# A state-space layer pair on one core: the taps' angle and magnitude matmuls read 128 rows, with zeros for the half that isn't theirs

## The chip, the cores and the metric

The kernel runs on one core of one Trainium2 chip. The time is device microseconds of that core, from launch to end, and the median of several runs counts. The profile is one further execution, taken by the hardware profiler. Its span is the time from the core's first instruction to its last.

A core has five engines with an instruction stream each: TensorE (PE, matmuls; its weight loads are shown apart as PEld), VectorE (DVE), ScalarE (ACT), GpSimd (POOL) and SyncE (SP, which here issues most transfers). Each works through its stream in order. TensorE's clock is granted by a gate, at half or full speed; the profile shows the granted share as PEclk.

## The reference, cut to what matters

The input is a sequence x of 2048 steps and 512 channels. Four layers follow each other, A, B, A, B, each on the layer norm of x and added to x:

```python
def A(q, k, v, shift_k, ssm_k, ssm_D):
    kv = shift_conv(k, shift_k) * v            # 4 taps
    return q * (causal_conv(kv, ssm_k) + kv * ssm_D)

def B(u, log_A_real, A_imag, C_real, C_imag, log_dt, D_skip):
    dt = exp(log_dt)                           # per channel d
    A = -exp(log_A_real) + 1j * A_imag         # [512 channels, 128 modes]
    C = (C_real + 1j * C_imag) * dt
    K[d, l] = 2 * sum_n Re(C[d, n] * exp(A[d, n] * dt[d] * l))
    return causal_conv(u, K) + u * D_skip
```

A's convolution doesn't depend on x (only its gate q does), and both layers A share it, as both layers B share the kernel K. So the filter K, called the taps here, has to be made once: 512 channels of 2048 values, each a sum over 128 modes.

## The kernel before, in words

The long convolutions are Fourier transforms written as matmuls. `fwd_group` with `fwd_rows` (L173) does the first step into a PSUM tile `pf`, VectorE transposes it (L191, L193), and `f2_chunk` (L198) does the second into `pu`. A filter's spectrum is copied out (`pc`, L249) and sent to DRAM as `spec`, by `spectrum_quarter`, a quarter of the channels at a time. `convolution` multiplies by it (L283 to L288) and goes back by L297 and L318.

The taps are made by `taps`, in 64 steps n = 4 gi + k: 16 groups gi of 32 channels, and in each group four steps k of 8 channels. Step k is split as `h, s = divmod(k, 2)`. All mode parameters are held as three 2-byte parts of each number with a fourth part of zero. `load_rows` brings a group's `rows` from DRAM: 128 rows for each h, of which rows 0 to 63 belong to the eight channels of s = 0 and rows 64 to 127 to those of s = 1. A matmul of these rows (128 modes as output partitions) with a small table (`tt`, `tg1`, `tg2`) gives 512 columns, one phase or exponent for each channel and position:

- `mags` (L486, `pm`): exponents. For `col == 2` it uses all 128 rows and table `tg2`, 16 channels at once; otherwise the 64 rows of one s and table `tg1`. ScalarE takes the exponential (L492, `m`).
- `angles` (L501, `pa`): phases by table `tt`, from the 64 rows of one s. VectorE rounds them to whole turns (L505, `y`), and L506 subtracts these on TensorE with the matrix `minus`.
- `waves` (L512 to L514): sine and cosine on ScalarE, in place in `pa` and into `co`.
- `products` (L524 to L528): wave by magnitude, on GpSimd and VectorE, into `xye`.
- `contract` (L538): sums over the modes by 32-column matmuls into `pk`; after four steps L547 and L548 scale the result, and it goes to DRAM as `kdram`.

`pm` and `pa` share three PSUM banks (NPA = 3). Exponentials are made for two groups at a time, so that ScalarE changes its tables seldom.

Two streams run together: `stream` (taps, and each quarter's spectrum of K as soon as 16 steps are done), one step at a time, and `diagonal`, two steps at a time. `diagonal` first makes the spectrum of A's filter in four quarters (`kk` from `ssmk_in`; the A transposes L191 write `x`), beside it the product kv on GpSimd (L636) and VectorE (L644, L646), and the row statistics (L655), and then runs A's convolution. The stage ends near 412 us; after it come A's gate, layer B, the second gate and the second layer B.

The order in which the instructions are written down is not the order in which they stand: a scheduler puts each engine's stream in order by its own model of what would be ready when. So a change of shape in one instruction can move others.

Of the kernel before, what the change touches and what calls it, by code (L numbers as in the profile page):

```python
# [79 lines left out]
def mode_constants():  # L80
    m = np.arange(32)
    n2 = np.concatenate([32 + m, 31 - m])
    tabs = {
        "tt": (8, np.concatenate([m + 1, 64 * m + 32]), np.repeat([0, 1], 32)),
        "tg1": (8, n2, 0 * n2),
        "tg2": (16, 64 * m, 0 * m + 1),
    }
    out = {}
    for name, (chans, rate, off) in tabs.items():
        t = np.zeros((2, 2, 8, 4, chans, len(rate)), np.float32)  # L90
        for s in range(2):
            for c in range(8):
                for r, factors in enumerate((rate, off)):
                    t[s, r, c, :3, (8 * s + c) % chans] = factors
        out[name] = t.reshape(128, chans, len(rate))
    out["minus"] = -np.eye(128, dtype=np.float32)
    return out
# [3 lines left out]
def kernel(ctx: ExitStack, tc: tile.TileContext, out, x_in, kv_in, ssmk_in, ssmd_in,  # L101
# [323 lines left out]
    split(3, t2, V)  # L425
    S.activation(warm, t2[:, 0, 0:1], AF.Exp, scale=0.0)
    tabs = {}
    for key, c_, w_, src in (("tg2", 16, 32, tg2_in), ("tg1", 8, 64, tg1_in), ("tt", 8, 64, tt_in)):
        tabs[key] = gp.tile([128, c_, w_], BF16, name=key)
        G.dma_start(tabs[key], src)  # L430
    nc.sync.dma_start(flat(dt2), ldtb_in[:, None, :].to_broadcast([4, 32, 128]))
# [35 lines left out]


    NR = 3
    rows, ms, pks, angs = {}, {}, {}, {}  # L470
    NM = 5
    last_exp, last_sin = [None], [None]
# [8 lines left out]

    def mags(gi, k, col):
        h, s = divmod(k, 2)
        hs = slice(0, 128) if col == 2 else slice(64 * s, 64 * s + 64)
        pm = pp.tile([128, 512], F32, name="pm", tag="pa", bufs=NPA)
        T.matmul(pm, rows[gi][hs, 1, h, :], tabs["tg2" if col == 2 else "tg1"][hs], start=True, stop=True)  # L486
        if col == 2:
            ms[gi, h] = wk.tile([128, 16, 96], F32, name="m", tag="m", bufs=NM)
            m = ms[gi, h][:, :, 64:96]
# [6 lines left out]

    def angles(gi, k):
        h, s = divmod(k, 2)
        hs = slice(64 * s, 64 * s + 64)
        pa = pp.tile([128, 512], F32, name="pa", tag="pa", bufs=NPA)  # L500
        T.matmul(pa, rows[gi][hs, 0, h, :], tabs["tt"][hs], start=True, stop=False,  # L501
                 skip_group_check=True)

        y = wk.tile([128, 512], F16, name="y", tag="y", bufs=2)
        V.tensor_scalar(y, pa, MAGIC, MAGIC, op0=ALU.add, op1=ALU.subtract)  # L505
        T.matmul(pa, minus, y, start=False, stop=True, skip_group_check=True)  # L506
        angs[gi, k] = pa
# [465 lines left out]
```

## Time and profile before

| | us |
|---|---|
| median of 3 runs | 711.91 |
| lowest and highest | 708.33, 714.90 |
| the profiled execution's own time | 715.19 |
| its span | 713.4 |
| TensorE busy (PE) | 574.0 |
| TensorE weight loads (PEld) | 392.5 |
| VectorE busy (DVE) | 522.5 |
| ScalarE busy (ACT) | 486.4 |
| GpSimd busy (POOL) | 461.5 |

The mean granted clock of TensorE was 0.935. A row of the profile reads: line, engine, operation, tile written <- tiles read, shapes, count, then busy time in us and the mean of one in ns, then idle time of the engine just before and what ended it. In a matmul's shape, `64*128` is rows by columns of the array in use, and `64x512` the moving operand. A matmul of 4-byte numbers shows as two records. A row of the timeline starts with start and length in us. A row of the windows gives from:to, length, then busy time and count of instructions of PE, PEld, DVE, ACT and POOL, the granted clock, the share of the transfer engines' time and GB/s.

### The profile page before, as it was taken

What the parts mean: (1) busy time and instruction counts of PE and PEld (TensorE: products, weight loads), DVE (VectorE), ACT (ScalarE), POOL (GpSimd) and SP (SyncE); (2) the same over time, 40 slices, a digit from 0 to 9 for tenths busy, and PEclk for the clock granted to TensorE, in tenths of its full rate; (3) what the DMA queues carried; (4) which work ended last, traced back from release to release, by engine and by line L of the source; (5) the groups of instructions that cost most, each with busy time, mean ns of one, the idle gap of its engine ahead of it and who ended that gap; (6) DMA issues with size and microseconds to landing.
All of it is one profiled execution on the core that took longest, in us unless ns stands there. A gap on an engine that the chain in (4) does not pass through costs nothing.

```text
span 713.4 us, 14266 instructions
## 1 busy us (share of the span) xinstructions
PE 574.0 (80%) x4984; PEld 392.5 (55%) x4984; DVE 522.5 (73%) x947; ACT 486.4 (68%) x886; POOL 461.5 (65%) x483
## 2 busy tenths in 40 slices
PE   1276876788898999989988977987898718689996
PEld 0043544445576786756745565766576304566783
DVE  7835878976585775674774878476797898988875
ACT  3435566658769868797898567986566375696572
POOL 5534989978758596595795522077668502787783
PEclk9999888967989999999999989999999959999999
DMA  8456968774773757746474795568786240577682
GB/s 285 164 168 203 348 210 289 234 252 146 231 223 105 206 137 191 214 131 196 125 206 138 218 325 168 177 177 240 190 220 169 64 123 1 147 182 213 194 224 103
DMA packets 84555, 134.44 MB, mean 188 GB/s; under 512 B 16892, under 2 KB 33924, under 8 KB 83332
## 3 DMA queue, kind: packets, MB, share of 16 engines
q1 hardware_dynamic: 83268, 131.01, 61.6%
q0 software_dynamic: 1216, 2.52, 1.4%
q8 instruction: 39, 0.64, 0.4%
q14 instruction: 32, 0.26, 0.1%
HBM read 98.28 MB, written 35.65 MB: 188 GB/s over the span
## 4 chain that ended last, share of the span: by engine, by line
PE 43%; ACT 15%; DVE 15%; DMA 13%; issue 7%; POOL 5%; SPq 2%; DVEq 0%; ACTq 0%; POOLq 0%
PE pu L198 15%; PE pf L173 11%; PE pi L297 6%; DMA kab<-spec 4%; PE po L318 4%; PE pk L538 3%; ACT u L818 2%; PE pm L486 2%; DMA spec<-pc 2%; POOL sw L287 2%; DVE x L755 2%; ACT co L514 1%; ACT sw L283 1%; PE pa L506 1%; DVE vv L285 1%
## 5 line engine op out<-in xcount | busy, mean ns | idle before, releaser
L287 POOL TENSOR_TENSOR sw<-sw,kab 128x512 f32<-128x512 f32 x96 | 125.7, 1315 | 70.2 <-ACT sw L284 58.7
L285 DVE TENSOR_TENSOR vv<-pu,kab 128x512 f32<-128x512 f32 x96 | 64.9, 679 | 67.1 <-ACT sw L284 46.2
L297 PE MATMUL pi<-vv,mm 128*128 128x128 f32 x768 | 104.2, 280 | 7.2 <-DVE vv L285 5.0
L297 PEld LDWEIGHTS pi<-vv,mm 128*128 128x128 f32 x768 | 93.9, 192 | 21.4 <-issue 11.2
L288 POOL TENSOR_TENSOR vv<-vv,sw 128x512 f32<-128x512 f32 x76 | 98.9, 1306 | 9.2 <-DVE vv L285 6.4
L283 ACT ACTIVATE sw<-pu 64x512 f32<-64x512 f32 x96 | 57.0, 594 | 61.7 <-PE pu L198 57.1
L173 PE MATMUL pf<-kk,wz 128*128 128x256 f32 (+1 forms) x176 | 64.0, 616 | 40.6 <-issue 17.3
L524 POOL TENSOR_TENSOR xye<-co,m 128x512 f32<-128x512 f32 x64 | 75.7, 1183 | 23.6 <-ACT co L514 15.2
L636 POOL TENSOR_TENSOR term<-kvt 128x512 f32<-128x512 f32 x64 | 81.9, 1299 | 12.0 <-ACT acc L642 9.0
L198 PE MATMUL pu<-x,w 128*128 128x128 f32 x512 | 81.3, 307 | 8.2 <-ACT pc L249 5.4
L198 PEld LDWEIGHTS pu<-zu,w 128*128 128x128 f32 x512 | 62.6, 190 | 43.1 <-DVE vv L285 17.6
L198 PEld LDWEIGHTS pu<-x,w 128*128 128x128 f32 x512 | 72.5, 215 | 24.0 <-issue 8.4
L198 PE MATMUL pu<-zu,w 128*128 128x128 f32 x512 | 72.7, 284 | 13.2 <-DVE vv L285 11.3
L173 PE MATMUL pf<-u,wz 128*128 128x256 f32 (+2 forms) x280 | 74.5, 478 | 3.6 <-DVE zu L191 2.5
L492 ACT ACTIVATE m<-pm 128x512 f32<-128x512 f32 x96 | 53.3, 608 | 19.0 <-PE pm L486 14.2
L512 ACT ACTIVATE co<-pa 128x512 f32<-128x512 f32 x64 | 38.5, 601 | 36.1 <-PE pa L506 35.9
L173 PEld LDWEIGHTS pf<-kk,wz 128*128 128x128 f32 (+1 forms) x176 | 30.0, 225 | 56.5 <-issue 43.5
L318 PE MATMUL po<-w,w 128*64 128x512 f32 x192 | 53.9, 643 | 8.4 <-DVE w L312 7.9
L249 ACT COPY pc<-pu 128x512 f32<-128x512 f32 x64 | 36.7, 585 | 30.6 <-PE pu L198 13.9
L538 PEld LDWEIGHTS pk<-xye 128*32 128x32 f32 x2048 | 35.6, 115 | 38.1 <-issue 14.1
L538 PE MATMUL pk<-xye 128*32 128x64 f32 x2048 | 48.9, 231 | 9.3 <-POOL xye L528 5.3
L284 ACT COPY sw<-pu 64x512 f32<-64x512 f32 x96 | 55.5, 578 | 1.1
(141 smaller groups left out, 1107.5 us busy)
## 6 DMA issues: line engine op xcount, KB each, us to landing
kab<-spec SPq DMA_DIRECT2D x188, 256.0 KB, 4.0
spec<-pc SPq DMA_DIRECT2D x64, 256.0 KB, 2.7
kvt<-kv_in SPq DMA_DIRECT2D x16, 624.0 KB, 5.6
yaq<-ya_d SPq DMA_DIRECT2D x5, 1024.0 KB
kk<-ssmk_in SPq DMA_DIRECT2D x16, 256.0 KB, 5.7
kv_d<-un SPq DMA_DIRECT2D x16, 256.0 KB, 2.9
xt<-x_in SPq DMA_DIRECT2D x16, 256.0 KB, 5.0
kdram<-ks SPq DMA_DIRECT2D x64, 64.0 KB, 3.2
```

Source lines behind the costliest of these rows:

```text
L173: yield T.matmul(o, w, rhs, start=True, stop=True)
L198: ins = T.matmul(pu[:, i, :], w2[:, c * CK + i, :], z[:, :, c * CK + i, :], start=True, stop=True)
L283: S.mul(sw[0:64], pu[64:128], -1.0)
L284: swapped[0] = S.copy(sw[64:128], pu[0:64])
L285: multiplied[0] = V.tensor_mul(vv, pu, kabs[s][:, 0])
L287: (V if last else G).tensor_mul(sw, sw, kabs[s][:, 1])
L288: (V if last or s % add_dve == add_dve - 1 else G).tensor_add(vv, vv, sw)
L297: i1s[t] = T.matmul(pi[:, i, :], mm[:, c * CK + i, :], vvs[t][:, i, :], start=True, stop=True)
L318: ins = T.matmul(po[64 * a:64 * a + 64], w4, ws[g][:, :, 16 * a:16 * a + 16, :].rearrange("p x t r -> p t x r"), start=True, stop=True, ti ...
L524: G.tensor_mul(xye[:, 0, :, 32:96], co[:, :, 1:65], m[:, :, 32:96])
L538: T.matmul(pk[32 * i4:32 * i4 + 32, 2 * k + i, :], xye[:, r, 4 * i + i4, 64:96], xye[:, r, 4 * i + i4, 0:64], start=r == 0, stop=r == 1, t ...
L636: G.tensor_mul(term, kvt[:, 3 - j:19 - j, :], tap(j))
```

## The change

The tables `tt` and `tg1` get 16 channels in place of 8: 1024 columns, in which the rows of one s are zero in the columns of the other. The table's entry for channel c of half s already went to column `(8 * s + c) % chans`, so only `chans` changes. `mags` and `angles` then take all 128 rows as stationary operand and the 512 columns of their own s. Sums get 64 products with zero in addition. Tables in SBUF and their loads double in size for these two. The loops over `WM` and `WA` run once.

```diff
-        "tt": (8, np.concatenate([m + 1, 64 * m + 32]), np.repeat([0, 1], 32)),
-        "tg1": (8, n2, 0 * n2),
+        "tt": (16, np.concatenate([m + 1, 64 * m + 32]), np.repeat([0, 1], 32)),
+        "tg1": (16, n2, 0 * n2),
...
-    for key, c_, w_, src in (("tg2", 16, 32, tg2_in), ("tg1", 8, 64, tg1_in), ("tt", 8, 64, tt_in)):
+    for key, c_, w_, src in (("tg2", 16, 32, tg2_in), ("tg1", 16, 64, tg1_in), ("tt", 16, 64, tt_in)):
...
+    WG = 6
+    WM = 1
+    WA = 1
...
-        hs = slice(0, 128) if col == 2 else slice(64 * s, 64 * s + 64)
         pm = pp.tile([128, 512], F32, name="pm", tag="pa", bufs=NPA)
-        T.matmul(pm, rows[gi][hs, 1, h, :], tabs["tg2" if col == 2 else "tg1"][hs], start=True, stop=True)
+        rhs = tabs["tg2"] if col == 2 else tabs["tg1"][:, 8 * s:8 * s + 8, :]
+        for _ in range(WM if gi < WG else 1):
+            T.matmul(pm, rows[gi][:, 1, h, :], rhs, start=True, stop=True)
...
-        hs = slice(64 * s, 64 * s + 64)
         pa = pp.tile([128, 512], F32, name="pa", tag="pa", bufs=NPA)
-        T.matmul(pa, rows[gi][hs, 0, h, :], tabs["tt"][hs], start=True, stop=False,
-                 skip_group_check=True)
+        for _ in range(WA if gi < WG else 1):
+            T.matmul(pa, rows[gi][:, 0, h, :], tabs["tt"][:, 8 * s:8 * s + 8, :], start=True, stop=False,
+                     skip_group_check=True)
```

No engine has an instruction more or less than before, and lines from L486 on stand four lower (L486 is L490 now, L501 is L505, L505 is L509). But the scheduler ordered the streams anew. TensorE's order differs from its first taps matmul to about 315 us of the trace and is the same from there on, and the other engines' orders differ over the same stretch and a little up to 450 us.

TensorE, at the start of the taps. Before, the first group's magnitudes (`pm`) stood ahead of the first two chunks of A's spectrum (`pu`):

```order
L486 MATMUL pm_306<-tg1_219,rw_296 128x512
L486 LDWEIGHTS rw_296
L486 MATMUL pm_309<-tg1_219,rw_296 128x512
L198 MATMUL pu_350<-x_254,w2_104 128x128 x4
L198 MATMUL pu_364<-x_254,w2_104 128x128 x4
```

TensorE at the same place now, from the last step ahead of it that is the same in both (`pf_290`):

```order
L173 MATMUL pf_290<-kk_287,wz_103 128x16x16x2 x2
L198 MATMUL pu_350<-x_254,w2_104 128x128 x4
L198 MATMUL pu_364<-x_254,w2_104 128x128 x4
L173 MATMUL pf_588<-kk_585,wz_103 128x16x16x2 x2
L490 LDWEIGHTS rw_296
L490 MATMUL pm_302<-tg2_217,rw_296 128x512
```

The two chunks and the next group's first Fourier step (`pf_588`) moved ahead of all magnitudes.

VectorE, in the third quarter of A's spectrum, before. `pf_1038` is the quarter's third group, and `pa` and `ks` are of the taps:

```order
L655 BN_STATS st0_108<-xt_1228 128x6
L211 BN_AGGR mv_107<-st0_108 128x2
L191 STREAM_TRANSPOSE x_254<-pf_1038 128x512 x2
L505 TENSOR_SCALAR y_617<-pa_615 128x512
L505 TENSOR_SCALAR y_674<-pa_672 128x512
L525 TENSOR_TENSOR xye0_247<-pa_548,m_324 128x8x64
```

VectorE at the transposes of the same group now:

```order
L509 TENSOR_SCALAR y_674<-pa_672 128x512
L648 TENSOR_TENSOR acc_762<-acc_762,term_722 128x512
L551 TENSOR_TENSOR ks_576<-pk_388,dt2_136 128x8x32
L552 TENSOR_TENSOR ks_576<-pk_388,dt2_136 128x8x32
L529 TENSOR_TENSOR xye1_249<-pa_615,m_324 128x8x64
L530 SCALAR_TENSOR_TENSOR xye1_249<-pa_615,m_324 128x8x31
L659 BN_STATS st0_108<-xt_1292 128x6
L191 STREAM_TRANSPOSE x_254<-pf_1038 128x512 x2
```

The transposes of `pf_1038` moved behind the rounding of `pa_672`, the first group's `ks` and the products of `pa_615`, 13 places later.

## The prediction

> **What bounds the kernel now.** I read the page's first two parts, then the chain of waits over the stage that the change touches (41.8 to 412 us, from the first tap matmul to just before the last), then that stage in windows as long as the steps in which the granted clock moves (3.41 us), and last single TensorE rows.
>
> ```profile
> span 713.4 us, 14266 instructions
> PEclk9999888967989999999999989999999959999999
> core 0: us, PE busy (x) PEld busy (x) DVE busy (x) ACT busy (x) POOL busy (x), PEclk, DMA share, GB/s
> 41.80:200.00 158.20, 127.91 (x1238) 78.86 (x1239) 115.73 (x217) 104.36 (x184) 121.81 (x128) 0.83 0.71 231
> by line: PE pu L198 17.0%; PE pf L173 13.8%; PE pk L538 6.0%; PE pi L297 5.8%; issue 5.5%; PE pm L486 4.1%; DMA spec<-pc 3.4%; ACT co L514 2.7%; PE pa L506 2.5%; PE po L318 2.5%; ACT m L492 2.3%; PE pa L501 2.3%; ACT co L512 2.2%; DMA kdram
> ```
>
> No engine is full here, but TensorE is nearest to it, and the last line (the chain over the stage, by line) gives it 17.0 + 13.8 + 6.0 + 5.8 + 4.1 + 2.5 + 2.5 + 2.3 = 54% of the stage. So a microsecond taken from TensorE is worth about 0.54. Up to 200 us it also runs at a mean granted clock of 0.83, which means a third of that time at half speed (1 - 0.83 = 0.17, twice that is 0.34).
>
> What makes the clock fall? Here are windows before a fall and just after it, and then two busy ones after which nothing fell:
>
> ```profile
> 157.01:160.42 3.41, 2.13 (x8) 0.57 (x8) 3.11 (x6) 1.78 (x2) 3.41 (x5) 1.00 0.79 260
> 160.42:163.84 3.42, 3.42 (x7) 1.09 (x7) 1.58 (x4) 3.41 (x8) 2.42 (x3) 0.50 0.51 180
> 163.84:167.25 3.41, 3.41 (x17) 3.04 (x15) 1.77 (x4) 2.29 (x5) 1.82 (x2) 0.50 0.50 180
> 191.14:194.56 3.42, 2.79 (x39) 1.18 (x39) 2.36 (x5) 3.42 (x8) 1.54 (x3) 1.00 0.77 256
> 194.56:197.97 3.41, 3.16 (x12) 2.20 (x12) 3.41 (x7) 2.38 (x4) 3.27 (x5) 0.50 0.45 141
> 197.97:201.38 3.41, 3.41 (x18) 3.34 (x18) 2.51 (x5) 2.55 (x5) 2.60 (x3) 0.50 0.89 236
> 218.45:221.86 3.41, 1.82 (x68) 0.94 (x56) 2.38 (x5) 3.38 (x7) 3.41 (x4) 1.00 0.44 123
> 314.02:317.44 3.42, 1.73 (x39) 0.81 (x37) 2.27 (x4) 3.38 (x7) 3.42 (x4) 1.00 0.04 9
> ```
>
> TensorE was busy 2.79 us in the window at 191.14 and the clock was halved behind it; at 314.02 it was busy 1.73 us and the clock stayed. Busy time alone doesn't decide. The groups of these two windows (three rows of 191.14, one of 314.02) differ in rows of the array:
>
> ```profile
> L538 PE MATMUL pk<-xye 128*32 128x64 f32 x32 | 1.2, 226 | 0.0
> L486 PE MATMUL pm<-tg,rw 64*128 64x512 bf16 x3 | 1.1, 382 | 0.4 <-ACT m L492 0.4
> L501 PE MATMUL pa<-tt,rw 64*128 64x512 bf16 x2 | 0.9, 474 | 0.2
> ...
> L318 PE MATMUL po<-w,w 128*64 128x512 f32 x6 | 1.7, 624 | 1.8 <-DVE w L312 1.7 <-DVE vv L285 0.2
> ```
>
> The window that lost the clock holds five of the 64-row matmuls, the other none. I took each matmul's streaming time from the starts of back-to-back ones of its shape (0.21 us for 512 columns of 2-byte numbers, twice that at half speed) and weighted it by the share of the array's rows and columns that it uses. Of the 16 windows after which the clock fell, 15 have a weight of at most 0.35 of the window and one 0.39; all that kept the clock have 0.36 or more. At half speed, windows up to 0.76 stayed there, and from 0.76 up they got the clock back. So here the gate follows the part of the array in use, and 64-row matmuls count half.
>
> **The change, part by part.**
>
> *Shape changes.* The matmuls of the two edited lines stand between 128-row ones:
>
> ```profile
> L486 PE MATMUL pm<-tg,rw x96: 372/387/631, 41.8 to 383.4; 64*128 64x512 bf16 x64, 128*128 128x512 bf16 x32
> L501 PE MATMUL pa<-tt,rw x64: 372/387/604, 57.3 to 402.2; 64*128 64x512 bf16 x64
> 127.60 0.39 PE L506 MATMUL pa<-y,minus 128*128 128x512 f16 x1
> 127.92 0.39 PE L501 MATMUL pa<-tt,rw 64*128 64x512 bf16 x1
> 128.24 1.16 PE L198 MATMUL pu<-x,w 128*128 128x128 f32 x8
> 131.60 0.38 PE L506 MATMUL pa<-y,minus 128*128 128x512 f16 x1
> 131.81 1.05 PE L198 MATMUL pu<-x,w 128*128 128x128 f32 x8
> ```
>
> From the 128-row L506 to L198 it is 131.81 - 131.60 = 0.21 us. Into the 64-row L501 it is 127.92 - 127.60 = 0.32, and out of it 128.24 - 127.92 = 0.32. A change of shape costs 0.10 us each way. I counted neighbours of different shape in TensorE's two orders, with the shapes of the trace: 421 before, 316 after. That is 105 x 0.10 = 10.5 us of TensorE's time, and by the chain's share 10.5 x 0.54 = 5.7 us saved (bounds: 0 if all of it lies beside other work, 10.5 if none does). The Trainium skill says in "TensorEngine Tiling (Array Packing)", Key Properties, that going to another tiling mode drains the engine; the rows agree, with 0.10 us a time.
>
> *Lost pairs.* Two 64-row matmuls on different halves of the array run side by side:
>
> ```profile
> 236.06 0.39 PE L501 MATMUL pa<-tt,rw 64*128 64x512 bf16 x2
> 236.38 0.83 PE L198 MATMUL pu<-x,w 128*128 128x128 f32 x5
> ```
>
> Two of them end in the 0.39 us of one. With all 128 rows they follow each other, and the second costs 0.21 us (the L506 to L198 step above). In the trace 24 such starts lie less than 40 ns behind another 64-row matmul, so 24 x 0.21 = 5.0 us of TensorE's time, and 5.0 x 0.54 = 2.7 us lost (0 to 5.0). The same page of the Trainium skill, under Key Properties, has tiles of different position work in parallel, which speaks against this change: by that rule, with all 128 of them paired, it would be 64 x 0.21 = 13.4 us, 7.3 on the chain, and the sum below would be 4.6 us worse. The trace shows 24 pairs.
>
> *The clock.* With 128 rows the weights above rise from 0.32 to 0.45 at 191.14 (clock kept), from 0.30 to 0.40 at 157.01 (kept, near the edge), and from 0.64 to 0.77 in the half-speed window at 40.96 (at the edge, back one step earlier). The chain inside the stretches that would no longer be slow, 44.37 to 47.78, 160.42 to 167.25 and 194.56 to 201.38, is nearly all TensorE:
>
> ```profile
> 42.93 3.71 PE pu L198 x16
> 161.36 2.00 PE pf L173 x2
> 163.36 3.72 PE pu L198 x16
> 196.42 5.11 PE pu L198 x24
> ```
>
> It adds up to 3.4 + 6.7 + 6.1 = 16.2 us, and at full speed would take half, so 8.1 us at most. Nothing less than 0 follows from the rows alone. As the new order shifts work between windows, I take two thirds, 5.4 us.
>
> *The start.* The first magnitudes now stand behind two chunks of L198 and two matmuls of L173:
>
> ```profile
> 37.90 1.31 DVE L191 STREAM_TRANSPOSE x<-pf 128x512 f32<-128x512 f32 x2 [2.23 <-PE pf L173]
> 41.78 1.15 PE L486 MATMUL pm<-tg,rw 128*128 128x512 bf16 x3 [3.92 <-DMA rw<-rows_d]
> 42.86 3.35 PE L198 MATMUL pu<-x,w 128*128 128x128 f32 x14
> ```
>
> Before, L198 was ready at 37.90 + 1.31 = 39.21 and stood behind L486, which waited for its rows until 41.78. Now it can fill that hole: up to 42.86 - 39.21 = 3.7 us gained by the A kernels' spectrum, while the magnitudes come about 39.21 + 3.7 + 1.6 - 41.78 = 2.7 us later (1.6 for the L173 pair by the chain). One stream gains what the other loses; I take 0, with -3.7 and +2.7 as ends.
>
> *The tables.* Two of the three table loads double.
>
> ```profile
> L430 POOL DMA_DIRECT2D tt<-tt_in x1: 568/568/568, 5.0 to 5.0; - x1
> 7.25 1.15 POOL L397 TENSOR_TENSOR la<-la,dtn 128x512 f32<-128x512 f32 x1 [1.68 <-ACT la L383]
> ```
>
> If issuing costs twice as much, that is 2 x 0.57 = 1.1 us on GpSimd, under the 1.68 us that it waits for ScalarE anyway; the data is not needed before 41.78. I take 0; without that cover it would be +1.1.
>
> *Sum.* -5.7 + 2.7 - 5.4 + 0 + 0 = -8.4 us. The profiled execution took 715.19 us (span 713.4) and would take 706.8. It stands 3.3 over the median of 711.91, so against the median I predict 711.9 - 8.4 = 703.5 us.
>
> **The rivals.** *The clock does not care for rows.* Then only the first two terms stay: 711.9 - 5.7 + 2.7 = 708.9 us. Against it speak the windows at 191.14 and 314.02; for it, that the two saved falls rest on few windows. The Trainium skill, "TensorE: Matmul & The Clock Gate", Part 1, says that the gate follows how busy TensorE was lately, which would be this rival. The busy times 2.79 (fell) and 1.73 (kept) don't fit that page as it stands.
>
> *The new order holds back the A spectrum.* The scheduler put the eleventh pair of A transposes (L191, just ahead of the first row here) 13 places later on VectorE.
>
> ```profile
> 85.47 1.25 DVE L505 TENSOR_SCALAR y<-pa 128x512 f16<-128x512 f32 x2
> 90.03 1.28 DVE L191 STREAM_TRANSPOSE x<-pf 128x512 f32<-128x512 f32 x2
> 91.87 0.60 DVE L547 TENSOR_TENSOR ks<-pk,dt 128x256 f32<-128x256 f32 x1
> 93.39 0.41 DVE L526 SCALAR_TENSOR_TENSOR xye<-pa,m 128x248 f32<-128x248 f32 x1
> ```
>
> The thirteen take from 85.47 to 93.80, less the stretch from 90.03 to 91.87 with four that stay behind: 8.3 - 1.8 = 6.5 us. If TensorE has nothing else ready, such a hole also costs the clock for two windows, as after 157.01, and 6.83 x 0.5 = 3.4 us. That gives 711.9 - 5.7 + 2.7 + 6.5 + 3.4 = 718.8 us, slower than before; with one window of slow clock or four it is 717 to 722. It decides from the point where the spectrum's chunks of that quarter, and not the taps, are what TensorE waits for. For it: this spectrum must end before convolution A begins. Against it: later L173 pairs stand 30 to 42 places earlier in TensorE's order, so the stream can catch up.
>
> *More gain.* All three stretches saved and the changes of shape wholly on the path: 711.9 - 10.5 + 2.7 - 8.1 = 696.0 us, and 693 with the start's 3.7 us nearly whole.
>
> **How the numbers follow.** Forecast 0.44, clock rival 0.22, order rival 0.27, more gain 0.07. The likeliest one's own range is 697 to 709. The range of 8 in 10 reaches from 693 (the last case) to 721 (the order rival but for its end). A measurement of this kernel can tell about 1%, 7.1 us, from no change. Faster by more (under 704.8): most of the forecast and the last case, 0.42. Within: the rest of the forecast, nearly all of the clock rival and the milder part of the order rival, 0.35. Slower (over 719.0): 0.17 of the order rival, and 0.06 from the first two cases, for moved instructions at places that I have not priced, 0.23.
>
> **What would show it.** Right: L486 and L501 start 0.21 us behind a 128-row neighbour, no two of them side by side; mean clock from 41.8 to 200 us well over 0.83; TensorE's busy time on the page lower than before. The clock rival: the same 0.83 with the shape changes gone. The order rival: VectorE's eleventh L191 pair near 91 us or later and convolution A starting late. Wrong altogether: a chain in which TensorE's share of the stage stays and the stage is no shorter, so that the freed time became waits for ScalarE.

## The result, and the profile after

The changed kernel is slower. Its median is 721.48 us (719.76 to 722.28, 4 runs) against 713.40 us of the kernel before beside it (708.33 to 715.59, 4 runs), a ratio of 1.0115 with a 95% interval of 1.0075 to 1.0156. I had forecast 703.5 us, in a range of 693 to 721. Here and below a median is over all runs, while a ratio leaves out runs more than 1.5% above the fastest of their kernel, so it isn't always the quotient of the two medians shown.

Line numbers of the kernel after: L486 of before is L490, L492 is L496, L501 is L505, L506 is L510, L524 and L528 are L528 and L532, L538 is L542, L636 is L640.

The head of the page of the kernel after, then its window from 41.8 to 200 us (columns as before), then its chain of waits from 41.8 to 412 us by line:

```profile
span 719.8 us, 14258 instructions
PE 571.2 (79%) x4984; PEld 393.9 (55%) x4984; DVE 522.6 (73%) x947; ACT 486.6 (68%) x886; POOL 461.9 (64%) x483
PEclk9998788867999999999999989999999969999998
41.80:200.00 158.20, 124.74 (x1244) 75.54 (x1244) 114.62 (x215) 105.56 (x188) 120.22 (x126) 0.85 0.70 230
by line: PE pu L198 11.0%; PE pf L173 10.8%; issue 8.3%; PE pk L542 5.5%; PE pi L297 4.6%; DMA xt<-x_in 3.3%; PE pm L490 3.1%; ACT co L516 2.9%; DMA spec<-pc 2.7%; POOL term L640 2.6%; ACT pa L517 2.5%; DVE acc L648 2.3%; PE po L318 2.3%; D
```

TensorE's work did become less: 571.2 us busy against 574.0, and in the window 124.7 against 127.9 at a clock of 0.85 against 0.83. In the first half of the span, the slices of the clock, 18 us each, are below 9 from the fourth to the tenth; before they were so in the fifth to seventh, the ninth, tenth and twelfth. So the falls moved more than they went. But TensorE's rows in the chain add up to 40%, where they were 54%: 11.0 + 10.8 + 5.5 + 4.6 + 3.1 + 2.3 = 37% in the line above, which shows only the longest, and 3% of L505 and L510. What TensorE gave up, others took: the transfer `xt`, GpSimd's `term`, VectorE's `acc`, and "issue". This alone doesn't make a kernel slower: in rows128_old_order below, which is faster, TensorE's rows add up to 41%.

The tile rows of the two edited lines, and two rows of TensorE's timeline:

```profile
L490 PE MATMUL pm<-tg,rw x96: 376/379/634, 44.2 to 387.7; 128*128 128x512 bf16 x96
L505 PE MATMUL pa<-tt,rw x64: 376/379/634, 57.5 to 406.6; 128*128 128x512 bf16 x64
123.73 0.39 PE L510 MATMUL pa<-y,minus 128*128 128x512 f16 x1
123.95 0.38 PE L505 MATMUL pa<-tt,rw 128*128 128x512 bf16 x1
```

The edit does what it says: all 160 matmuls have 128 rows, one starts 123.95 - 123.73 = 0.22 us behind a 128-row neighbour (0.32 before), and none starts beside another. The first magnitudes come at 44.2 us (41.8 before), the last at 387.7 (383.4), the last angles at 406.6 (402.2). So the stage ends about 4.4 us later, although TensorE's busy time is less. The span is 6.4 us longer (719.8 against 713.4), so about 2 us more are lost behind the stage. Where these come from isn't shown.

Where? The exponentials on ScalarE are good milestones, because all 96 keep their order. I count them from 0. These rows give the first and last start of exponentials 12 to 18, 36 to 48 and 60 to 71 (ahead of the colon their number, then min/median/max ns), for the kernel after and then for the kernel before:

```profile
L496 ACT ACTIVATE m<-pm x7: 597/603/617, 92.3 to 102.8; 128x512 f32<-128x512 f32 x7
L496 ACT ACTIVATE m<-pm x13: 597/621/668, 182.0 to 223.6; 128x512 f32<-128x512 f32 x13
L496 ACT ACTIVATE m<-pm x12: 592/597/603, 272.9 to 296.2; 128x512 f32<-128x512 f32 x12
```

```profile
L492 ACT ACTIVATE m<-pm x7: 597/618/662, 100.2 to 105.0; 128x512 f32<-128x512 f32 x7
L492 ACT ACTIVATE m<-pm x13: 592/619/685, 183.9 to 223.4; 128x512 f32<-128x512 f32 x13
L492 ACT ACTIVATE m<-pm x12: 592/600/657, 274.5 to 289.0; 128x512 f32<-128x512 f32 x12
```

They take 10.5, 41.6 and 23.3 us in the kernel after, and 4.8, 39.5 and 14.5 in the kernel before. At the start of the first group the changed kernel is 7.9 us ahead (92.3 against 100.2), at the end of the third it is 7.2 behind (296.2 against 289.0). It loses in each group, and most in the third.

### The profile page after: what moved, and what is told of

Read it like the earlier page. It is cut to its first block, busy times and chain, and to the rows that moved or that the text cites. A ratio compares the mean times of both kernels' runs of the same rounds, so it can differ in the third digit from the quotient of the medians.

```text
span 719.8 us, 14258 instructions
## 1 busy us (share of the span) xinstructions
PE 571.2 (79%) x4984; PEld 393.9 (55%) x4984; DVE 522.6 (73%) x947; ACT 486.6 (68%) x886; POOL 461.9 (64%) x483
## 4 chain that ended last, share of the span: by engine, by line
PE 40%; DVE 15%; ACT 15%; DMA 12%; issue 9%; POOL 7%; SPq 2%; DVEq 0%; POOLq 0%; ACTq 0%
PE pu L198 13%; PE pf L173 10%; PE pi L297 6%; PE po L318 5%; DMA kab<-spec 3%; PE pk L542 3%; ACT u L822 2%; POOL sw L287 2%; DMA xt<-x_in 2%; PE pm L490 2%; ACT pc L249 1%; DVE w L312 1%; ACT co L516 1%; ACT sw L283 1%; DVE x L759 1%
## 5 line engine op out<-in xcount | busy, mean ns | idle before, releaser
L287 POOL TENSOR_TENSOR sw<-sw,kab 128x512 f32<-128x512 f32 x96 | 125.6, 1314 | 76.9 <-ACT sw L284 62.8
L297 PEld LDWEIGHTS pi<-vv,mm 128*128 128x128 f32 x768 | 96.3, 196 | 21.4 <-issue 11.5
L288 POOL TENSOR_TENSOR vv<-vv,sw 128x512 f32<-128x512 f32 x76 | 98.8, 1304 | 8.3 <-DVE vv L285 5.5
L283 ACT ACTIVATE sw<-pu 64x512 f32<-64x512 f32 x96 | 57.1, 595 | 60.0 <-PE pu L198 57.5
L640 POOL TENSOR_TENSOR term<-kvt 128x512 f32<-128x512 f32 x64 | 82.2, 1300 | 20.6 <-ACT acc L646 11.5
L173 PE MATMUL pf<-kk,wz 128*128 128x256 f32 (+1 forms) x176 | 63.0, 607 | 39.8 <-issue 13.3
L528 POOL TENSOR_TENSOR xye<-co,m 128x512 f32<-128x512 f32 x64 | 75.6, 1180 | 19.3 <-ACT co L518 12.5
L198 PE MATMUL pu<-x,w 128*128 128x128 f32 x512 | 79.0, 302 | 10.2 <-ACT pc L249 7.3
L198 PEld LDWEIGHTS pu<-zu,w 128*128 128x128 f32 x512 | 62.7, 191 | 41.6 <-DVE vv L285 15.6
L173 PE MATMUL pf<-u,wz 128*128 128x256 f32 (+2 forms) x280 | 74.5, 477 | 3.6 <-DVE zu L191 2.5
L249 ACT COPY pc<-pu 128x512 f32<-128x512 f32 x64 | 37.0, 589 | 40.2 <-PE pu L198 23.3
L516 ACT ACTIVATE co<-pa 128x512 f32<-128x512 f32 x64 | 38.4, 600 | 37.8 <-PE pa L510 37.2
L496 ACT ACTIVATE m<-pm 128x512 f32<-128x512 f32 x96 | 53.0, 608 | 10.9 <-PE pm L490 10.0
L173 PEld LDWEIGHTS pf<-kk,wz 128*128 128x128 f32 (+1 forms) x176 | 28.7, 221 | 56.9 <-issue 37.3
L542 PEld LDWEIGHTS pk<-xye 128*32 128x32 f32 x2048 | 36.7, 117 | 40.1 <-issue 19.3
L542 PE MATMUL pk<-xye 128*32 128x64 f32 x2048 | 50.8, 234 | 8.2 <-POOL xye L532 5.5
```

The source lines that it names most:

```text
L173: yield T.matmul(o, w, rhs, start=True, stop=True)
L198: ins = T.matmul(pu[:, i, :], w2[:, c * CK + i, :], z[:, :, c * CK + i, :], start=True, stop=True)
L283: S.mul(sw[0:64], pu[64:128], -1.0)
L287: (V if last else G).tensor_mul(sw, sw, kabs[s][:, 1])
L288: (V if last or s % add_dve == add_dve - 1 else G).tensor_add(vv, vv, sw)
L297: i1s[t] = T.matmul(pi[:, i, :], mm[:, c * CK + i, :], vvs[t][:, i, :], start=True, stop=True)
```

## The experiments

The names of the instructions are the same in both kernels, so one kernel can be built with the other's order. All 18 runs below do this:

```diff
+def keep_order(nc, tc):
+    for names in ORDER:                      # one list for each engine
+        for first, then in zip(names, names[1:]):
+            tc.add_manual_dep(nc.get_inst_by_name(f"I-{then}"), f"I-{first}",
+                mybir.DependencyInfo(mybir.DependencyClass.NoSync, mybir.DependencyReason.DATA),
+                reason="order")
...
+        keep_order(nc, tc)
```

Such an edge makes the scheduler place `then` behind `first` on the same engine. It adds no semaphore: with before's order written down in this way and 64-row matmuls (wide_tables_64_old_order), the trace has the same number of instructions as that of the kernel before (14266), semaphore instructions among them (1446), in the same order on every engine. Orders were joined only where both have issued the same instructions on an engine, at the place nearest to the named time in the trace of before. "Old" below is the order of the kernel before, "new" that of the kernel after. Every median has a ratio to the kernel before, run beside it (11 to 34 runs).

### Rows and order apart

```diff
 rows128_old_order:         matmuls as changed (128 rows)
-order: new
+order: old
 rows64_new_order:          order: new
-matmuls with 128 rows
+matmuls with 64 rows and narrow tables, as before
 wide_tables_64_old_order:  tables as changed, order: old
-matmuls with 128 rows
+matmuls with 64 rows
```

> 128-row taps matmuls with wide tables, but every engine's stream held in the order that it had before the change. Theory (the new order is what costs, the rows themselves gain): faster than before by the sum of my first three terms, 5.7 - 2.7 + 5.4 = 8.4 us, so a ratio near 0.988, and at least by the first two, 3.0 us (0.996); TensorE changes shape 105 times less, mean granted clock from 41.8 to 200 us above 0.83. Rival (the 128-row matmuls cost, by the pairs that no longer run side by side, or by the tables): as slow as the changed kernel, 1.0115.

> The kernel of before, 64-row matmuls and small tables, held in the order that the changed kernel has. Theory (order): slower than the changed kernel, since it has the new order's cost without the rows' gain: ratio to before 1.015 to 1.025. Rival (rows): no slower than before, 1.00.

> 64-row matmuls as before, but with the wide tables and their longer loads, in before's order. The prediction priced the tables at 0 with +1.1 us as an end. If the tables cost nothing and the gain of 128 rows in before's order (0.9956) comes from the rows alone: 0.998 to 1.002. If the tables cost their 1.1 us, which the rows would then have had to make up for: 1.0015 and over.

| run | median us (runs) | ratio | 95% interval |
|---|---|---|---|
| rows128_old_order | 712.45 (12) | 0.9956 | 0.9925 to 0.9986 |
| rows64_new_order | 727.21 (6) | 1.0139 | 1.0084 to 1.0193 |
| wide_tables_64_old_order | 714.77 (12) | 0.9994 | 0.9961 to 1.0028 |
| the changed kernel | 721.48 (4) | 1.0115 | 1.0075 to 1.0156 |

So the rows gain 0.44%, some 3.2 us. The order that came with them costs about 1.6% at 128 rows (1.0115 against 0.9956) and 1.4% at 64. The tables cost nothing that can be measured, and neither does writing an order down (wide_tables_64_old_order has both). The slowdown is the order's. rows128_old_order reached only what my first two terms were to give (0.996), not the 0.988 of all three.

The rows also do for the clock what I said. Two windows, of rows128_old_order and of rows64_new_order:

```profile
41.80:200.00 158.20, 120.12 (x1243) 73.37 (x1242) 115.31 (x216) 103.52 (x182) 121.53 (x127) 0.89 0.70 228
41.80:200.00 158.20, 130.42 (x1221) 77.17 (x1222) 112.54 (x212) 102.21 (x180) 118.87 (x123) 0.77 0.68 223
```

With before's order the clock goes from 0.83 to 0.89, with the new one from 0.77 (64 rows) to 0.85 (128). So the new order costs clock as well. In runs made side by side, the mean granted clock was 0.9162 in the 6 of rows64_new_order and 0.9316 in the 29 of the kernel before.

The three groups of exponentials of rows128_old_order:

```profile
L496 ACT ACTIVATE m<-pm x7: 597/617/655, 96.7 to 101.6; 128x512 f32<-128x512 f32 x7
L496 ACT ACTIVATE m<-pm x13: 591/617/681, 184.3 to 221.7; 128x512 f32<-128x512 f32 x13
L496 ACT ACTIVATE m<-pm x12: 591/600/652, 272.4 to 286.5; 128x512 f32<-128x512 f32 x12
```

4.9, 37.4 and 14.1 us: against these the changed kernel's order loses 5.6, 4.2 and 9.2.

### Which stretch of the order

```diff
 128 rows in all; order:
+rows128_new_then_old:  new to 230 us, old behind
+rows128_old_then_new:  old to 230 us, new behind
+rows128_new_to_97:     new to 97 us, old behind
+rows128_new_97_230:    old, new from 97 to 230 us, old
+rows128_new_182_230:   old, new from 180 to 230 us, old
+rows128_new_272_298:   old, new from 272 to 298 us, old
+rows128_new_from_298:  old to 298 us, new behind
```

> The changed kernel with its new order up to about 230 us of the trace and the order of before from there on. In the trace of the changed kernel the taps are 2 to 3 us ahead of before at 230 us and 5 us behind at 325. If the order between is what costs, this one keeps the lead: ratio 0.993 to 0.998. If the loss there is of the rows (pairs lost, clock), it stays: 1.01.

> The changed kernel with the order of before up to about 230 us and its new order from there on. Order theory: whatever lead the rows give by 230 us, less the 7.5 us that the new order loses between 250 and 325: 1.000 to 1.012, and slower than the kernel with the order of before throughout by about 7 us. Rows theory: as the changed kernel, 1.01, and no different from the others with 128 rows.

> 128 rows, and before's order everywhere but from about 272 to 298 us (the exponentials of the fourth set of steps and the inverse transforms' copies ahead of the first Abs of steps 40 on), where the changed kernel's order stands. 128 rows with all of before's order measured 0.9956 of the kernel before, and with the new order from 230 us on 1.0034, so 0.0078 (5.6 us) are lost somewhere from 230 us on. Theory A: they are lost here, since ScalarE takes its copies ahead of the exponentials and waits for TensorE between them (7.9 us of waits from 281 to 298 us in the changed kernel's trace, 4.8 in the same work of before's order): 1.003, with ScalarE's last exponential of this set 4 to 6 us later than its first step leads one to expect. Rival B: the loss is made behind the first Abs: 0.996. Rival C: the new order of 230 to 272 us only moves work from this stretch into that one, and this part of it alone gains or loses by itself: 0.990 or below, or 1.007 and over.

> 128 rows, before's order up to about 298 us and the changed kernel's order behind it. Theory A (the loss is made in the waits ahead of the first Abs, 272 to 298 us): 0.996. Rival B (it is made behind the first Abs, in the waits of 1.2, 1.3 and 0.6 us that ScalarE has at 315 to 319 us with the new order and has not with the old): 1.003. In between, 0.999, if both take part.

> 128 rows, the changed kernel's order up to about 97 us and before's order behind it. With the new order to 230 us it was 0.9995, with none of it 0.9956. In the changed kernel's trace the work up to 97 us is 5 to 8 us ahead of the kernel before, and between 98 and 130 us this lead is gone. Theory A: the lead is real and the order of the next stretch wastes it; with before's order there, 4 to 8 us of it stay: 0.985 to 0.990, which would be the best kernel so far. Rival B: the lead is only work taken first that the other stream of work then lacks, so it is paid back whatever the order behind: 0.9956 to 0.9995. Rival C: the new order's first part is the one that loses: over 1.000.

> 128 rows, the changed kernel's order from about 97 to 230 us and before's order ahead and behind. Theory A (the lead up to 97 us is real and this stretch wastes it): without the lead the stretch costs 8 to 12 us against before's order, 1.006 to 1.012. Rival B (what the changed kernel loses from 98 to 130 us is the price of work taken first): nothing has been taken first here, so 0.993 to 0.998.

> 128 rows, the changed kernel's order from about 180 to 230 us and before's order elsewhere. In the traces the time from the 36th to the 48th exponential is 41.1 to 41.6 us in every kernel with the new order there and 37.0 to 38.0 in every other with 128 rows. Theory A: this order makes a loss of its own of 4 us: 0.9956 + 4/715 = 1.001, and 41 us between those exponentials. Rival B: it is the late part of what was lost ahead of it (work left over): 0.993 to 0.998, and 37 to 38 us.

| run | median us (runs) | ratio | 95% interval | the three groups, us |
|---|---|---|---|---|
| rows128_old_order (above) | 712.45 | 0.9956 | 0.9925 to 0.9986 | 4.9, 37.4, 14.1 |
| rows128_new_then_old | 716.53 (12) | 0.9995 | 0.9957 to 1.0033 | 10.2, 41.1, 14.1 |
| rows128_old_then_new | 718.68 (12) | 1.0034 | 1.0001 to 1.0066 | 4.9, 38.0, 23.3 |
| rows128_new_to_97 | 709.80 (12) | 0.9946 | 0.9915 to 0.9976 | 8.4, 37.4, 14.1 |
| rows128_new_97_230 | 721.09 (12) | 1.0099 | 1.0068 to 1.0130 | 13.2, 41.5, 14.1 |
| rows128_new_182_230 | 716.76 (12) | 1.0020 | 0.9987 to 1.0054 | 4.9, 42.8, 14.1 |
| rows128_new_272_298 | 717.45 (12) | 1.0042 | 1.0006 to 1.0078 | 4.9, 37.0, 23.3 |
| rows128_new_from_298 | 716.16 (12) | 0.9997 | 0.9964 to 1.0031 | 4.9, 37.3, 14.1 |

The last column is the better instrument for the place. With before's order it repeats, whatever stands ahead: 4.9, 37.0 to 38.0 and 14.1 us. Each group is long where its stretch has the new order, and nowhere else (the first group lies across the cut at 97 us). It doesn't say how much the kernel loses, since ScalarE does other work between the exponentials. 272 to 298 us alone costs 0.0086 over before's order, which was theory A of that run. 180 to 230 us alone costs 0.0064, 4.6 us, also theory A. rows128_new_then_old lies between its two cases. Behind 298 us there may be a little more (0.0041, with the interval of before's order overlapping). The lead up to 97 us is mostly given back by itself: with before's order behind it, 0.9946 is no better than 0.9956 can tell, so there theory A fell.

rows128_new_to_97 is the fastest measured, ahead of both kernels; whether it is better than rows128_old_order stays open.

What do the engines do at these places? At the first, ScalarE and SyncE's queue in the kernel after, then the same copy and SyncE's queue in rows128_old_order:

```profile
96.51 1.58 ACT L496 ACTIVATE m<-pm 128x512 f32<-128x512 f32 x3
101.83 0.59 ACT L249 COPY pc<-pu 128x512 f32<-128x512 f32 x1 [3.73 <-DMA spec<-pc]
96.64 6.12 SPq L250 DMA_DIRECT2D spec<-pc  x2
```

```profile
102.72 0.59 ACT L249 COPY pc<-pu 128x512 f32<-128x512 f32 x1 [0.56 <-DMA spec<-pc]
97.80 2.31 SPq L250 DMA_DIRECT2D spec<-pc  x2
```

In the kernel after, the copy of a part of the spectrum waits 3.73 us until the one before it has left its buffer, and the exponentials stand behind that copy. In the old order the same copy waits 0.56 us. A queue row of two issues reaches from the start of the first to the end of the second. In the kernel after, the second issue is that of the waiting copy itself, and stands behind it; in the old order both issues are of copies ahead. Without the lead (rows128_new_97_230) the same order waits elsewhere, on TensorE:

```profile
104.99 2.39 PE L173 MATMUL pf<-kk,wz 64*128 64x512 f32 x4 [5.62 <-DMA kk<-kdram]
107.31 1.46 PE L490 MATMUL pm<-tg,rw 128*128 128x512 bf16 x3
```

L173, moved ahead of the magnitudes, stands 5.62 us in front of its load, with the magnitudes behind it.

At the third place, ScalarE's waits in the kernel after, then all of those in rows128_old_order, from 281 us on up to the change of table ahead of the first sine:

```profile
281.77 0.59 ACT L283 ACTIVATE sw<-pu 64x512 f32<-64x512 f32 x1 [2.25 <-PE pu L198]
286.86 1.15 ACT L496 ACTIVATE m<-pm 128x512 f32<-128x512 f32 x2 [1.82 <-PE pm L490]
288.72 0.59 ACT L249 COPY pc<-pu 128x512 f32<-128x512 f32 x1 [0.72 <-PE pu L198]
289.70 0.59 ACT L283 ACTIVATE sw<-pu 64x512 f32<-64x512 f32 x1 [0.39 <-PE pu L198]
294.30 0.59 ACT L283 ACTIVATE sw<-pu 64x512 f32<-64x512 f32 x1 [1.14 <-PE pu L198]
298.38 0.59 ACT L249 COPY pc<-pu 128x512 f32<-128x512 f32 x1 [1.59 <-PE pu L198]
```

```profile
281.48 0.59 ACT L283 ACTIVATE sw<-pu 64x512 f32<-64x512 f32 x1 [2.23 <-PE pu L198]
284.90 1.08 ACT L496 ACTIVATE m<-pm 128x512 f32<-128x512 f32 x2 [0.16 <-PE pm L490]
291.36 0.59 ACT L283 ACTIVATE sw<-pu 64x512 f32<-64x512 f32 x1 [2.37 <-PE pu L198]
```

The new order takes chunks of the convolution ahead of the last magnitudes. ScalarE waits six times, 7.9 us, where it waited 4.8, and the last exponential, behind which its table changes, starts at 296.2 instead of 286.5. Part of that is work taken earlier: the change of table itself, behind the same work but for one copy, starts at 299.48 instead of 293.87, 5.6 us later.

### Single steps put back

That suggested two culprits: the early L173 at the first place, the late magnitudes at the third. In each run one of them is put back where the old order has it.

```diff
 128 rows in all; order:
 rows128_new_97_230_pf_back:     as rows128_new_97_230, but
-  97 to 126 us: L173 and its transposes L191 at their new places
+  97 to 126 us: L173 and its transposes L191 at their old places
 rows128_new_272_298_taps_back:  as rows128_new_272_298, but
-  272 to 298 us: the taps' instructions at their new places
+  272 to 298 us: the taps' instructions at their old places
 new_order_taps_back:            all new, with the second of these edits
 new_order_both_back:            all new, with both
```

> As the run with the changed kernel's order from 97 to 230 us and before's order elsewhere (1.0099), but from 97 to 126 us the L173 matmuls of the A spectrum and the transposes that read them stand where before's order has them, behind the magnitudes' matmuls. In the trace of that run TensorE stood 5.62 us in front of the first of them, for its part of the kernel (kk<-kdram), with six magnitude matmuls behind it whose rows were there, and ScalarE 5.84 us behind those. Theory A: an engine that takes its work in order and stands at a transfer costs this much, so with the L173 back most of the 0.0143 goes: 0.995 to 1.001. Rival B: the transfers are late in any order and the wait only moves to the next instruction that needs one (the kernel spectrum's copies L249 and their DMA): 1.006 to 1.010.

> As the run with the changed kernel's order from 272 to 298 us (1.0042), but the taps' own instructions (magnitudes, exponentials, angles, contraction) stand there where before's order has them relative to the convolution's; the rest of the stretch keeps the new order. Theory A: the loss is that the magnitudes' matmuls come behind two more chunks of the convolution, so that ScalarE waits for TensorE between them and its last exponential, on which the change of its table for Abs and Sin waits, comes late: 0.993 to 0.999, back at the 0.9956 of before's order. Rival B: the loss lies in the convolution's own new order (copies L283, L284 and L298 and the loads kab): 1.003 to 1.006.

> The changed kernel with its whole order, but for 272 to 298 us, where the taps' instructions stand as in before's order. If the two losses are independent and the taps' late place is the second one (theory A), 1.0115 falls by the 0.0086 that this stretch cost alone: 1.001 to 1.005. If the delay is made anyway because the kernel is bound elsewhere by then (rival B), 1.008 to 1.012.

> The run before this one, and from 97 to 126 us the L173 matmuls and their transposes as in before's order too. Alone, with before's order ahead of it, the new order from 97 to 230 us cost 0.0143, with the new order ahead only 0.0049 (0.9995 against 0.9946). If L173's place is the cause in both (theory A), this run is 0.003 to 0.006 below the one before it, 0.996 to 1.001. In the changed kernel's own trace, though, L173 waits 0.74 us there, and TensorE and ScalarE stand 3.9 and 3.7 us later, at the copy L249 that waits for the transfer of the copy before it (256 KB, 5.1 us from issue to landing). If that is another cause (rival B), the L173's return gains nothing: equal to the run before within 0.003.

| run | median us (runs) | ratio | 95% interval | the three groups, us |
|---|---|---|---|---|
| rows128_new_97_230_pf_back | 730.31 (6) | 1.0180 | 1.0114 to 1.0245 | 11.6, 41.6, 14.1 |
| rows128_new_272_298_taps_back | 722.43 (12) | 1.0075 | 1.0036 to 1.0114 | 4.9, 38.3, 17.7 |
| new_order_taps_back | 719.33 (12) | 1.0066 | 1.0024 to 1.0109 | 9.3, 41.6, 16.2 |
| new_order_both_back | 725.85 (6) | 1.0132 | 1.0073 to 1.0190 | 10.2, 41.9, 16.2 |

Theory A fell in the first, second and fourth, and the third lies between the two theories. L173 back was slower than L173 early (1.0180 against 1.0099; with the whole new order 1.0132 against 1.0066), which neither theory had. The two intervals overlap in each pair, but both pairs go the same way. The taps back shorten the third group from 23.3 to 17.7 and 16.2 us, but alone the run is no faster than with the new order there (1.0075 against 1.0042). Only in the whole new order do they help, 1.0115 to 1.0066, with overlapping intervals. So I could not name one moved instruction as the cause.

The orders written into these kernels say more than the names of the runs. With the taps at their old places, TensorE, ScalarE and VectorE have before's order over the whole stretch from 272 to 298 us. What is left of the new one are 22 places of GpSimd and 17 of SyncE. So the convolution's own instructions don't change their order on the first three engines, and what rows128_new_272_298_taps_back loses against before's order is the work of GpSimd's and SyncE's new order alone. (The profiled execution of new_order_both_back, from which its three groups are read, took 733.69 us, 7.8 more than its median.)

### Which engine's order

What else could hold TensorE and ScalarE? In two places GpSimd's new order puts other work (the gate's `term` L640, the spectrum's add L241 that waits for a load, the convolution's `sw` and `vv`, L287 and L288) ahead of the taps' products (L528, L532), which the contraction needs. So engines were set apart.

```diff
 128 rows in all; order: old on every engine, but
+early_sp_pool_only:         SyncE and GpSimd new, 97 to 126 us
+late_dve_sp_pool_only:      VectorE, SyncE and GpSimd new, 272 to 298 us
+pool_new_from_97:           GpSimd new, from 97 us on
 order: new on every engine, but
+new_order_pool_old_97_230:  GpSimd old, 97 to 230 us
```

> 128 rows and before's order, but from 97 to 126 us the order of SyncE and GpSimd (transfers issued, and GpSimd's products) is the changed kernel's; TensorE, ScalarE and VectorE keep before's. The new order from 97 to 230 us on all engines measured 1.0099, before's order 0.9956, and in its trace 8.3 us of the difference came between the 12th and the 18th exponential (13.2 us against 4.9). Theory A: the loss is in the order in which SyncE and GpSimd issue the spectrum's loads and the gate's work, which is why the L173's return didn't help: 1.003 to 1.010, and 8 us or more from the 12th to the 18th exponential. Rival B: it is in the order of the computing engines: 0.993 to 0.999, and about 5 us there.

> 128 rows and before's order, but from 272 to 298 us VectorE, SyncE and GpSimd have the changed kernel's; TensorE and ScalarE keep before's. The new order there on all engines measured 1.0042, 23.3 us from the 60th to the 71st exponential against 14.1 of before's order. Theory A: the loss is in TensorE's and ScalarE's order, in which convolution chunks stand ahead of the magnitudes and copies ahead of the exponentials: 0.993 to 0.999, and 14 to 15 us for those exponentials. Rival B: it is in the order of the transfers and of the products: 1.002 to 1.007.

> 128 rows and before's order on every engine but GpSimd, which from 97 us on has the changed kernel's order: the gate's products (L640), the spectrum's adds that wait for a load (L241) and the convolution's products (L287, L288) further ahead, the taps' products (L528, L532) behind them. Theory A: GpSimd's order alone makes the losses, since the taps' contraction waits for its products: 1.005 to 1.015, with 41 us or more from the 36th to the 48th exponential (37.4 in before's order) and 20 us or more from the 60th to the 71st (14.1). Rival B: the losses need the new order of TensorE, ScalarE or the transfer queue: 0.993 to 0.999, with 37 to 38 and 14 to 15 us.

> The changed kernel with its whole order, but GpSimd's from 97 to 230 us, which is before's. Theory A (GpSimd's order makes the losses at 98 to 113 us and 185 to 224 us): 37 to 38.5 us from the 36th to the 48th exponential (41.6 in the changed kernel) and 0.999 to 1.007, the late loss of 5 to 6 us being left. Rival B (the other engines' orders make them too, or GpSimd's old order does not fit theirs and waits in its turn): 41 to 42 us there, 1.009 and over.

| run | median us (runs) | ratio | 95% interval | the three groups, us |
|---|---|---|---|---|
| early_sp_pool_only | 721.78 (6) | 1.0108 | 1.0060 to 1.0155 | 7.7, 37.0, 14.1 |
| late_dve_sp_pool_only | 721.53 (6) | 1.0104 | 1.0053 to 1.0155 | 4.9, 37.3, 21.6 |
| pool_new_from_97 | 735.13 (6) | 1.0254 | 1.0201 to 1.0307 | 8.2, 42.9, 21.9 |
| new_order_pool_old_97_230 | 733.06 (6) | 1.0263 | 1.0220 to 1.0307 | 14.7, 47.9, 23.3 |

In the second run rival B won: with TensorE and ScalarE in the old order, the third group still takes 21.6 us. (Its profiled execution is one of its quickest, span 710.6 us; that lies ahead of this group.) GpSimd and TensorE of late_dve_sp_pool_only show how:

```profile
262.88 2.48 POOL L288 TENSOR_TENSOR vv<-vv,sw 128x512 f32<-128x512 f32 x2
265.32 1.17 POOL L528 TENSOR_TENSOR xye<-co,m 128x512 f32<-128x512 f32 x1
266.45 0.68 POOL L532 TENSOR_TENSOR xye<-co,m 128x256 f32<-128x256 f32 x1
267.19 1.08 PE L542 MATMUL pk<-xye 128*32 128x64 f32 x32 [5.85 <-POOL xye L532]
```

The convolution's products go first on GpSimd, and TensorE stands 5.85 us at the contraction. With the other engines in the old order, GpSimd's new order alone is enough to make the second and third group long. The second and third group of pool_new_from_97, and its TensorE at the same contraction:

```profile
L496 ACT ACTIVATE m<-pm x13: 591/616/679, 186.9 to 229.8; 128x512 f32<-128x512 f32 x13
L496 ACT ACTIVATE m<-pm x12: 588/597/615, 280.6 to 302.6; 128x512 f32<-128x512 f32 x12
282.27 1.08 PE L542 MATMUL pk<-xye 128*32 128x64 f32 x32 [5.82 <-POOL xye L532]
```

42.9 and 22.0 us, as theory A had it and near the changed kernel's 41.6 and 23.3; the ratio of 1.0254 is beyond it. But this is not how the changed kernel loses its time. Over the whole trace, TensorE's contraction L542 stands idle for GpSimd's product L532 for 26.6 us in pool_new_from_97, but for 5.5 us in the kernel after and 7.8 us in rows128_old_order.

At the second place the taps' product comes behind an add that waits for a load and behind the gate's terms. These rows of GpSimd show it in the kernel after. Then follow the add ahead of this one in rows128_new_182_230, which waits longer, with four terms behind it, and last, in rows128_old_order, the same product and add as in the kernel after, with the product ahead:

```profile
199.02 0.24 POOL L241 TENSOR_TENSOR kk<-kk,dr 1x32 f32<-1x32 f32 x1 [2.24 <-DMA kk<-kdram]
199.22 1.26 POOL L640 TENSOR_TENSOR term<-kvt 128x512 f32<-128x512 f32 x1
200.82 1.18 POOL L528 TENSOR_TENSOR xye<-co,m 128x512 f32<-128x512 f32 x1
```

```profile
192.24 0.24 POOL L241 TENSOR_TENSOR kk<-kk,dr 1x32 f32<-1x32 f32 x1 [5.71 <-DMA kk<-kdram]
192.45 4.94 POOL L640 TENSOR_TENSOR term<-kvt 128x512 f32<-128x512 f32 x4
```

```profile
200.04 1.19 POOL L528 TENSOR_TENSOR xye<-co,m 128x512 f32<-128x512 f32 x1 [0.59 <-ACT co L518]
202.93 0.24 POOL L241 TENSOR_TENSOR kk<-kk,dr 1x32 f32<-1x32 f32 x1 [1.05 <-DMA kk<-kdram]
```

Here too it isn't shown that this makes the loss: the contraction that follows the product waits for it only 0.46 us in the kernel after and 0.26 us in rows128_new_182_230.

The reverse does not mend the kernel either. With GpSimd's old order put into the changed kernel (new_order_pool_old_97_230), the groups get longer still, 14.7 and 47.9 us: theory A fell there, and rival B, that GpSimd's old order does not fit the others' new one, fits the numbers. The same goes for early_sp_pool_only: its ratio is about theory A's, but only 2.8 us of its loss lie in the first group, and 9.9 behind it (30.3 us from exponential 18 to the twelfth L516, 20.4 in the old order). That is a loss that the changed kernel doesn't have.

What is shown, then: the new order makes the loss, and it holds the taps at three places. GpSimd's part of it, alone, holds them at the second and third too, but by a wait that the changed kernel doesn't have. What stays open: by which wait the changed kernel loses the time, and which engine's order one would have to mend. Every mixture of two engines' orders within a stretch was slower than before's order. That the orders fit each other would explain it, but no run shows it by itself.

## Why the prediction was wrong

- **The moved instructions at places not priced** are the step that failed. The sum held no term for them, and they got 0.06 of chance. They cost 1.6%, some 11 us, by the comparison of the changed kernel with rows128_old_order (1.0115 against 0.9956). That is more than the whole forecast gain of 8.4 us. How the order makes the loss is open in part, as said above.
- **The order rival** had the direction and nearly the time (718.8 us), but not the place, so the nearness is luck. VectorE's tenth, eleventh and sixteenth pair of L191 in A's spectrum:

```profile
67.25 1.29 DVE L191 STREAM_TRANSPOSE x<-pf 128x512 f32<-128x512 f32 x2
85.81 1.30 DVE L191 STREAM_TRANSPOSE x<-pf 128x512 f32<-128x512 f32 x2
129.53 1.30 DVE L191 STREAM_TRANSPOSE x<-pf 128x512 f32<-128x512 f32 x2
```

  Before, they stood at 76.50, 84.27 and 138.31 us. So the eleventh pair, which I watched, was held back, but out of a lead of 9 us, to 85.81 and not to 91, and the last pair stood 8.8 us earlier than before. Convolution A started as before, at 216.5 us against 216.3 (its first L283). It was not A's spectrum that came late; it was the taps.
- **"Later L173 pairs stand 30 to 42 places earlier, so the stream can catch up"** came out for A's spectrum, by those 8.8 us. But it looked at one stream only, and an earlier place is no gain by itself. In rows128_new_97_230 the earlier L173 stood 5.62 us in front of its load, with the magnitudes behind it. That this is what the order costs is not shown: with L173 put back the kernel was no faster.
- **Shape changes and lost pairs** came as said in mechanism: 0.22 us between neighbours, no pairs. Their sum of -3.0 us lies in what 128 rows gain in the old order, 3.2 us (1.0 to 5.4), but the clock's gain is in these 3.2 us too. Shape changes, pairs and clock were not measured apart.
- **The clock** did rise, by as much as I took or more, but apparently at a third to a half of the price. The mean granted clock of the runs was 0.9424 with rows128_old_order (12 runs) against 0.9316 of the kernel before beside it (29 runs): 0.0108 x 713 = 7.7 us of clock, where my term took 5.4. But the three terms together were to give 8.4 us, and 3.2 were measured, 5.4 at most by the interval. The clock term is mis-sized. I had counted the chain inside the slow stretches as lost in full. Over 107 runs of the kernel before, of five sets, each taken against its own mean, the time falls by 1.8 us (1.1 to 2.5) for each 0.01 of mean clock, that is for 7.1 us of clock: a quarter. By this, 0.0108 is worth 1.9 us. With all 120 runs of these sets it is 2.5 us (1.7 to 3.2) for each 0.01, a third, and 0.0108 is worth 2.7 us. That is a correlation; no run changed the clock alone.
- **The start** came as its two ends said: the first magnitudes 2.4 us later (2.7 forecast), and the A spectrum's first copy 3.9 us earlier (41.67 against 45.55 us at its end; 3.7 forecast). **The tables** cost nothing measurable (0.9994).
- **The sign that I had named for "wrong altogether"** came, in part: the stage is no shorter and the freed time became waits. They are waits for transfers and GpSimd too, not only for ScalarE.

## What to carry to other kernels

Where a scheduler sets the order, a change of an instruction's shape is two changes, and the second can be over three times the first, with the other sign. Hold the old order, measure the shape alone, and then decide whether the new order is wanted. Don't expect to mend the new order by taking one engine's order, or one group of instructions, from the old one: here no such mixture was as fast as the old order.

## What I had not expected

- Orders mixed by engine were worse than either pure one: GpSimd's order alone, put new into the old one from 97 us on, gave 1.0254, and put old into the new one from 97 to 230 us 1.0263, where the pure orders have 0.9956 and 1.0115.
- A microsecond of lost clock went with only a quarter to a third of a microsecond of time in this kernel, though TensorE is the busiest engine and has 54% of the chain.
- The same transfer of 256 KB by SyncE, the one for which the copy at the first place waits, took 5.1 us from issue to landing in the kernel after (96.64 to 101.73) and 2.8 us in rows128_old_order (99.79 to 102.62).
